# Gated attention, ELU layer and SwiGLU layer on one core: the first two chunks of layer one divided in halves, and the positive part of ELU made by ScalarE

## The chip, the cores and the metric

The kernel runs on one core of a Trainium2 chip, as one program launched once. The metric is device time in microseconds (us), the median over runs of the same program. The engines of the core are named as in the profile: PE (TensorE's matrix products), PEld (its weight loads), DVE (VectorE), ACT (ScalarE), POOL (GpSimd) and SP (SyncE, whose queue issues every DMA here).

## What is computed

Three stages follow one another, all in float32:

```
for t in range(S):                                   # attention, B=4, H=8, S=768, D=48
    state = alpha[t][:, None] * state + outer(k[t], v[t])
    y[t]  = q[t] @ state
x = y as 3072 tokens x 384
h = x @ w_in                                         # layer one, 384 -> 2048 -> 384
x = where(h > 0, h, exp(min(h, 0)) - 1) @ w_out
g = x @ w_gate                                       # layer two, 384 -> 1536 -> 384
out = (g * sigmoid(g) * (x @ w_val)) @ w_out2
```

## The kernel before

Tokens are worked on in six chunks of 512 (128 steps of the sequence for each of four batches). Attention is cut into 24 units, one for each chunk and batch, so four units make the input x of one chunk. The seven steps of a unit u stand in a list called `queue`, in the order A(u+1), E(u), N(u+1), Gs(u), M(u+1), Hy(u), Dk(u+1), and `pop(n)` emits the next n of them. The last one of a unit that writes x is Hy (lines 291 to 321; ACT lines 317 and 318 copy the high part, DVE lines 319 and 320 make the low part). After the fourth unit of a chunk, `gaps` moves rows of x with six small DMAs (x<-x, line 337), and only then is x complete. Unit u+3 is loaded when unit u is done, since there are three input buffers. After the first chunk, Dk, Gs and Hy of all units share one PSUM bank (`aps`).

Layer one of a chunk has 16 steps f, one for each 128 hidden features. `mm1(f)` multiplies x by a column block into a PSUM tile h (two buffers), in nine matmuls, since each float32 product is made of three passes over parts split in two. ELU then runs as a chain: ACT relu of -h (L361), ACT exp (L362), DVE minus one (L363), DVE max(h, 0) plus that (L364), ACT copy to the high part g (L366), DVE subtraction to the low part (L367). `mm2(f)` multiplies g into the three accumulators acc0 to acc2, again nine matmuls; it is emitted two steps late, through `pend`. After f=15 the accumulators are copied by ACT, DVE and ACT (L383, L381) into tiles o and stored to DRAM, from where layer two reads them.

Each of the 16 weight blocks of layer one arrives packed, is decoded by `value` (two ACT, two DVE operations, L91 to L98) and split by `split` (one ACT, one DVE, L105 and L106). `p1.step()` emits the split of one block and the decoding of the next; a raw block's load waits for the split that frees one of two buffers. `mm1(f)` and `mm2(f)` use blocks 2(f//2) and 2(f//2)+1. Before layer one starts, the four units of chunk 0 are emitted with three steps of `p1` among them; then one step follows each f of chunk 0:

```
for c in range(NCH):
    for f in range(NF1):
        mm1(f)
        pend.append((mm2, f))
        if c == 0:
            p1.step()
        ...
        pop(POPS[f])          # POPS = [3] * 9 + [1] + [0] * 6: 28 a chunk, the four units of chunk c+1
        if len(pend) > 2:
            m, ff = pend.pop(0)
            m(ff)
```

The program's order is not the engines' order: a planner places the instructions of all engines by their readiness in its own timing, the earlier emitted first among those that are ready, and the order on each engine is then fixed. Layer two's 18 weight blocks are prepared in the same way from the end of chunk 4 on, during chunk 5 and the first chunk of layer two.

Of the kernel before, what the change touches and what calls it, by code (L numbers as in the profile page):

```python
# [33 lines left out]
EARLY = 10  # L34
POPS = [3] * 9 + [1] + [0] * 6
PASSES = ((0, 0), (0, 1), (1, 0))
# [3 lines left out]
def kernel(  # L40
# [14 lines left out]
    def open_pools(es, weights):  # L55
        P.wp = es.enter_context(tc.tile_pool(name="wp", bufs=weights))
        P.xp = es.enter_context(tc.tile_pool(name="xp", bufs=2))
        P.ep = es.enter_context(tc.tile_pool(name="ep", bufs=2))
        P.gp = es.enter_context(tc.tile_pool(name="gp", bufs=3))
        P.rp = es.enter_context(tc.tile_pool(name="rp", bufs=AHEAD))  # L60
        P.op = es.enter_context(tc.tile_pool(name="op", bufs=2))

    dp = ctx.enter_context(tc.tile_pool(name="dp", bufs=1, space=bass.MemoryType.DRAM))
    x2d = [dp.tile([128, KD, TB], F32, name=f"x2d{c}") for c in range(NCH)]

# [57 lines left out]
    class Attention:  # L123
# [167 lines left out]
        def Hy(self, u):  # L291
# [11 lines left out]
            for p, cs in enumerate(cols):  # L303
# [6 lines left out]
                    start=not c and p == 0, stop=p == NP - 1,  # L310
                )
            x = xt[c]
            ts = slice(b * C, (b + 1) * C)
# [33 lines left out]

    def moe1(x, w1, pacc, ph, put):

# [3 lines left out]
        def mm1(f):  # L353
# [3 lines left out]
            for kk in range(KD):  # L357
                mm3(h, lambda a: w[:, a, kk, fs], lambda b: x[:, b, kk], kk == 0, kk == KD - 1)
            e = P.ep.tile([128, TB], F32, tag="e", name="e")
            g = P.gp.tile([128, 2, TB], F32R, tag="g", name="g")  # L360
            nc.scalar.activation(out=e, in_=h, func=AF.Relu, scale=-1.0)  # L361
            nc.scalar.activation(out=e, in_=e, func=AF.Exp, scale=-1.0)  # L362
            nc.vector.tensor_scalar(out=e, in0=e, scalar1=-1.0, scalar2=None, op0=ALU.add)  # L363
            nc.vector.scalar_tensor_tensor(  # L364
                out=e, in0=h, scalar=0.0, in1=e, op0=ALU.max, op1=ALU.add)
            nc.scalar.activation(out=g[:, 0], in_=e, func=AF.Copy)  # L366
# [4 lines left out]
        def mm2(f):  # L371
            w = as_rows(w1[f // G, 1])
            g = gh.pop(f)
            for m in range(KD):
                mm3(acc[m], lambda a: w[:, a, f % G, m * 128:(m + 1) * 128],
                    lambda b: g[:, b], f == 0, f == NF1 - 1)
            if f == NF1 - 1:
                for m in range(KD):
                    o = P.op.tile([128, TB], F32, tag="o", name="o")
                    if m == 1:  # L380
                        nc.vector.tensor_copy(o, acc[m])  # L381
                    else:
                        nc.scalar.activation(out=o, in_=acc[m], func=AF.Copy)  # L383
                    nc.sync.dma_start(out=put(m), in_=o)
# [99 lines left out]
    for u in range(NU):  # L484
# [3 lines left out]
        def finish(u=u):  # L488
            c, b = divmod(u, B)
            if b == B - 1:  # L490
                at.gaps(c, 0, B)
                if c + 1 < NCH:
                    new_x(c + 1)
            if u + 3 < NU:
# [24 lines left out]
    at.init()  # L519
    new_x(0)  # L520
    at.A(0)
# [3 lines left out]
    for i in range(B):  # L525
        pop(7)
        if i:
            p1.step()

    pend = []  # L530
    for c in range(NCH):
        mm1, mm2 = moe1(xt[c], w1, pacc, ph, lambda m, c=c: x2d[c][:, m])
        for f in range(NF1):
            mm1(f)
            pend.append((mm2, f))
            if c == 0:
                p1.step()
            if p2 and f * EARLY // NF1 < (f + 1) * EARLY // NF1:
                p2.step()
            pop(POPS[f])  # L540
            if len(pend) > 2:
                m, ff = pend.pop(0)
                m(ff)
            if c == NCH - 1 and f == 4:
                x_next = load_split(lambda m: x2d[0][:, m])
# [182 lines left out]
```

## Time and profile before

| | us |
|---|---|
| median of three runs | 1021.77 (1021.47 to 1023.0) |
| the profiled execution, device time | 1022.64 |
| its span, first to last instruction | 1020.9 |
| PE busy in the span | 980.6 |
| DVE busy | 573.5 |
| ACT busy | 462.7 |
| mean granted clock of PE, share of full speed | 0.974 |

The span and the device time differ by 1.7 us, and the profiled execution stands 0.87 us above the median. A busy PE is not a PE at its peak, since the ends of matmuls are modelled; the spacing of starts and the number of matmuls say more.

### The profile page before, as it was taken

How to read it: one execution, taken by the hardware profiler on the slowest of the kernel's cores; microseconds unless marked ns; L12 is line 12 of the kernel's file. 1: busy time of each engine (PE TensorE's matmuls, PEld its weight loads, DVE VectorE, ACT ScalarE, POOL GpSimd, SP SyncE). 2: the span in 40 equal slices, each digit the busy share in tenths (PEclk: the TensorE clock that was granted, in tenths of full speed). 3: DMA queues.
4: the chain of work that ended last, by engine and by line, in shares of the span. 5: the costliest groups of instructions: out<-in, count | busy, mean ns of one | idle time of the engine just before them, and what ended most of it. 6: DMA issues, size and time to landing. Idle time of an engine off the chain costs nothing.

```text
span 1020.9 us, 13174 instructions
## 1 busy us (share of the span) xinstructions
PE 980.6 (96%) x5248; PEld 813.9 (80%) x5248; DVE 573.5 (56%) x951; ACT 462.7 (45%) x806; POOL 86.2 (8%) x59
## 2 busy tenths in 40 slices
PE   7589999999999999999998999999999999999997
PEld 4467778877787878888776888888888888888886
DVE  6899996656665665647888433433433433433332
ACT  5678786455555455637877321211311222212121
POOL 4223111120211121100000000000000000000000
PEclk8589999999999999999999999999999999999998
DMA  5544432222112212203533100100200100100001
GB/s 227 206 160 165 165 120 74 83 57 73 43 55 75 83 42 58 73 16 125 186 124 125 62 1 1 62 1 1 62 1 1 62 1 1 62 1 22 10 0 35
DMA packets 18934, 69.36 MB, mean 68 GB/s; under 512 B 2480, under 2 KB 5552, under 8 KB 15920
## 3 DMA queue, kind: packets, MB, share of 16 engines
q1 hardware_dynamic: 18864, 68.43, 19.9%
q8 instruction: 43, 0.70, 0.3%
q14 instruction: 27, 0.22, 0.1%
HBM read 56.62 MB, written 9.44 MB: 65 GB/s over the span
## 4 chain that ended last, share of the span: by engine, by line
PE 79%; DVE 8%; DMA 7%; ACT 3%; issue 2%; SPq 0%; POOL 0%; DVEq 0%
PE gv L117 29%; PE q L117 15%; PE acc L117 14%; PE h L117 14%; DMA raw<-w 4%; DMA in<-qkva 2%; PE ape L254 2%; DVE wt L106 2%; PE aps L299 2%; PE aps L308 1%; DVE raw L98 1%; DVE raw L95 1%; DVE in L195 1%; ACT raw L93 1%; ACT raw L91 1%
## 5 line engine op out<-in xcount | busy, mean ns | idle before, releaser
L117 PE MATMUL gv<-x,wt 128*128 128x512 f32 x1296 | 310.1, 393 | 2.3 <-DVE e L364 2.3
L117 PEld LDWEIGHTS gv<-x,wt 128*128 128x128 f32 x1296 | 243.3, 189 | 51.0 <-issue 2.7
L117 PE MATMUL acc<-g,wt 128*128 128x512 f32 x864 | 224.6, 398 | 4.3 <-DVE g L367 2.4
L117 PE MATMUL h<-x,wt 128*128 128x512 f32 x864 | 220.3, 398 | 8.4 <-DVE e L364 4.2
L117 PEld LDWEIGHTS h<-x,wt 128*128 128x128 f32 x864 | 161.3, 190 | 45.5 <-DVE e L364 6.6
L117 PEld LDWEIGHTS acc<-g,wt 128*128 128x128 f32 x864 | 158.7, 188 | 44.0 <-DVE g L367 4.4
L117 PE MATMUL q<-wt,u 128*128 128x384 f32 x864 | 163.0, 337 | 0.0
L117 PEld LDWEIGHTS q<-wt,u 128*128 128x128 f32 x864 | 153.6, 188 | 5.5
L414 DVE TENSOR_TENSOR s<-gv,s 128x512 f32<-128x512 f32 x72 | 49.8, 692 | 180.9 <-ACT s L413 180.8
L413 ACT ACTIVATE s<-gv 128x512 f32<-128x512 f32 x72 | 43.1, 598 | 185.3 <-PE gv L117 185.2
L416 ACT ACTIVATE u<-s 128x512 fp32r<-128x512 f32 x72 | 45.4, 631 | 130.4 <-DVE s L415 130.4
L366 ACT ACTIVATE g<-e 128x512 fp32r<-128x512 f32 x96 | 60.2, 629 | 65.6 <-DVE e L364 64.1
L361 ACT ACTIVATE e<-h 128x512 f32<-128x512 f32 x96 | 56.7, 590 | 58.7 <-PE h L117 57.8
L367 DVE TENSOR_TENSOR g<-e,g 128x512 fp32r<-128x512 f32 x96 | 67.8, 708 | 16.5 <-ACT g L366 15.0
L363 DVE TENSOR_SCALAR e<-e 128x512 f32<-128x512 f32 x96 | 42.6, 446 | 61.2 <-ACT e L362 61.0
L417 DVE TENSOR_TENSOR u<-s,u 128x512 fp32r<-128x512 f32 x72 | 49.8, 692 | 44.0 <-ACT u L416 44.0
L415 DVE TENSOR_TENSOR s<-gv,s 128x512 f32<-128x512 f32 x72 | 49.8, 691 | 43.0 <-PE gv L117 43.0
L364 DVE SCALAR_TENSOR_TENSOR e<-h,e 128x512 f32<-128x512 f32 x96 | 65.9, 687 | 2.1
L224 POOL TENSOR_TENSOR in<-in 112x512 f32<-112x512 f32 x24 | 40.6, 1691 | 300.2 <-DVE in L195 266.5
L362 ACT ACTIVATE e<-e 128x512 f32<-128x512 f32 x96 | 59.9, 628 | 1.8
L195 DVE TENSOR_TENSOR_SCAN in<-in,zero 112x128 f32<-112x128 f32 x96 | 34.5, 415 | 26.8 <-DMA in<-qkva 26.8
L214 POOL TENSOR_TENSOR in<-in,R 112x512 f32<-112x512 f32 x24 | 43.6, 1818 | 35.7 <-ACT R L204 35.6
(88 smaller groups left out, 776.0 us busy)
## 6 DMA issues: line engine op xcount, KB each, us to landing
raw<-w SPq DMA_DIRECT2D x34, 768.0 KB, 4.3
in<-qkva SPq DMA_DIRECT2D x23, 1024.0 KB, 5.0
x2d<-o SPq DMA_DIRECT2D x18, 256.0 KB, 2.0
x2r<-x2d SPq DMA_DIRECT2D x18, 256.0 KB, 2.9
out<-y SPq DMA_DIRECT2D x24, 192.0 KB, 2.0
x<-x SPq DMA_DIRECT2D x36, 64.0 KB, 4.5
in<-qkva SPq DMA_DIRECT2D x1, 768.0 KB, 5.1
in<-qkva SPq DMA_DIRECT2D x1, 256.0 KB, 3.7
```

The lines of the kernel that those rows point to most:

```text
L117: nc.tensor.matmul(out=o, lhsT=lhs(a), rhs=rhs(b), start=first and i == 0, stop=last and i == 2,)
L195: nc.vector.tensor_tensor_scan(out=f, data0=f, data1=self.zero[0:PR].to_broadcast([PR, C]), initial=1.0, op0=ALU.mult, op1=ALU.add,)
L214: nc.gpsimd.tensor_tensor(out=k, in0=k, in1=d["R"], op=ALU.mult)
L361: nc.scalar.activation(out=e, in_=h, func=AF.Relu, scale=-1.0)
L362: nc.scalar.activation(out=e, in_=e, func=AF.Exp, scale=-1.0)
L364: nc.vector.scalar_tensor_tensor(out=e, in0=h, scalar=0.0, in1=e, op0=ALU.max, op1=ALU.add)
L366: nc.scalar.activation(out=g[:, 0], in_=e, func=AF.Copy)
L367: nc.vector.tensor_tensor(out=g[:, 1], in0=e, in1=f32(g[:, 0]), op=ALU.subtract)
L414: nc.vector.tensor_tensor(out=e, in0=ps[0], in1=e, op=ALU.mult)
L415: nc.vector.tensor_tensor(out=e, in0=ps[1], in1=e, op=ALU.mult)
L416: nc.scalar.activation(out=g[:, 0], in_=e, func=AF.Copy)
L417: nc.vector.tensor_tensor(out=g[:, 1], in0=e, in1=f32(g[:, 0]), op=ALU.subtract)
```

## The change

The work of layer one is cut into segments. Chunk 0's steps f=0 to 7 come first, then chunk 1's f=0 to 7, then chunk 0's f=8 to 15, then chunk 1's f=8 to 15, then chunks 2 to 5 whole. A segment that ends at f=7 stores its three accumulators to a DRAM tile `half`; the segment that ends at f=15 loads them into three o tiles when f=12 is reached, and DVE adds the accumulators to them before the store. The four units of chunk 1 are emitted in the first segment, four steps for each of seven f; the second and third segment have none; the units of chunk 2 come in the fourth. One step of `p1` follows each f of the first four segments, and two, not three, come before layer one. x of a chunk is allocated at its first Hy. In ELU, ACT makes relu(h) into a tile r (one buffer), the DVE operation L363 is gone, and L364 reads r and e in SBUF instead of h in PSUM. The o tiles get a third buffer.

```diff
-POPS = [3] * 9 + [1] + [0] * 6
+HALF = NF1 // 2
+FULL = [3] * 9 + [1] + [0] * 6
+SEGMENTS = [(0, 0, HALF, [4] * 7 + [0]), (1, 0, HALF, [0] * 8),
+            (0, HALF, NF1, [0] * 8), (1, HALF, NF1, [4] * 7 + [0])]
+SEGMENTS += [(c, 0, NF1, FULL) for c in range(2, 6)]
...
-        P.op = es.enter_context(tc.tile_pool(name="op", bufs=2))
+        P.op = es.enter_context(tc.tile_pool(name="op", bufs=3))
...
+    half = [dp.tile([128, KD, TB], F32, name=f"half{c}") for c in range(2)]
...
+            if b == 0:
+                new_x(c)
...
+            r = P.ep.tile([128, TB], F32, tag="r", name="r", bufs=1)
             nc.scalar.activation(out=e, in_=h, func=AF.Relu, scale=-1.0)
+            nc.scalar.activation(out=r, in_=h, func=AF.Relu)
             nc.scalar.activation(out=e, in_=e, func=AF.Exp, scale=-1.0)
-            nc.vector.tensor_scalar(out=e, in0=e, scalar1=-1.0, scalar2=None, op0=ALU.add)
             nc.vector.scalar_tensor_tensor(
-                out=e, in0=h, scalar=0.0, in1=e, op0=ALU.max, op1=ALU.add)
+                out=e, in0=e, scalar=-1.0, in1=r, op0=ALU.add, op1=ALU.add)
...
-                    lambda b: g[:, b], f == 0, f == NF1 - 1)
-            if f == NF1 - 1:
+                    lambda b: g[:, b], f == f0, f == f1 - 1)
+            if f == f1 - 1:
                 for m in range(KD):
-                    o = P.op.tile([128, TB], F32, tag="o", name="o")
-                    if m == 1:
+                    o = part[m] if part else P.op.tile([128, TB], F32, tag="o", name="o")
+                    if part:
+                        nc.vector.tensor_tensor(out=o, in0=acc[m], in1=o, op=ALU.add)
+                    elif m == 1:
...
-        if i:
+        if i > 1:
             p1.step()
...
-    for c in range(NCH):
-        mm1, mm2 = moe1(xt[c], w1, pacc, ph, lambda m, c=c: x2d[c][:, m])
-        for f in range(NF1):
+    for c, f0, f1, pops in SEGMENTS:
+        to = half[c] if f1 < NF1 else x2d[c]
+        part = []
+        mm1, mm2 = moe1(xt[c], w1, pacc, ph, lambda m, to=to: to[:, m], f0, f1, part)
+        for f in range(f0, f1):
...
-            if c == 0:
+            if c < 2:
                 p1.step()
...
-            pop(POPS[f])
+            pop(pops[f - f0])
...
+            if f0 and f == f0 + 4:
+                for m in range(KD):
+                    t = P.op.tile([128, TB], F32, tag="o", name="part")
+                    nc.sync.dma_start(out=t, in_=half[c][:, m])
+                    part.append(t)
```

## Rows read from the trace of the kernel before

**Rows 1.** The page's part 1: busy us of each engine over the span.

```profile
PE 980.6 (96%) x5248; PEld 813.9 (80%) x5248; DVE 573.5 (56%) x951; ACT 462.7 (45%) x806; POOL 86.2 (8%) x59
```

**Rows 2.** Windows: stretch, length; busy us (instructions) PE, PEld, DVE, ACT, POOL; clock, DMA.

```profile
56.00:156.00 100.00, 96.43 (x577) 75.81 (x578) 93.85 (x153) 79.07 (x137) 20.62 (x11) 0.96 0.45 154
242.00:328.00 86.00, 86.00 (x529) 68.54 (x529) 53.69 (x102) 46.66 (x91) 13.92 (x8) 1.00 0.20 63
470.00:570.00 100.00, 92.34 (x386) 72.21 (x385) 79.94 (x116) 77.29 (x116) 0.00 (x0) 0.98 0.37 129
```

**Rows 3.** Timeline of ACT, the chunks' first copy of acc0: start, duration, instruction.

```profile
156.00 0.60 ACT L383 ACTIVATE o<-acc 128x512 f32<-128x512 f32 x1
...
240.65 0.60 ACT L383 ACTIVATE o<-acc 128x512 f32<-128x512 f32 x1 [0.22 <-PE acc L117]
...
326.73 0.60 ACT L383 ACTIVATE o<-acc 128x512 f32<-128x512 f32 x1 [0.23 <-PE acc L117]
```

**Rows 4.** Timeline of PE: layer one's first matmuls, and four groups in chunk 1.

```profile
56.09 2.90 PE L117 MATMUL h<-x,wt 128*128 128x512 f32 x6 [3.93 <-DMA x<-x]
...
197.61 2.23 PE L117 MATMUL h<-x,wt 128*128 128x512 f32 x9
199.68 2.20 PE L117 MATMUL acc<-g,wt 128*128 128x512 f32 x9
201.72 2.20 PE L117 MATMUL h<-x,wt 128*128 128x512 f32 x9
203.76 0.39 PE L117 MATMUL acc<-g,wt 128*128 128x512 f32 x1
```

**Rows 5.** Windows of tile e alone: busy us of DVE, of ACT; clock, DMA.

```profile
56.00:156.00 100.00, 31.38 (x51) 31.22 (x52) 0.96 0.45 154
```

**Rows 6.** Windows of tile raw alone (weight blocks): busy us of DVE, of ACT.

```profile
56.00:156.00 100.00, 36.05 (x37) 30.76 (x35) 0.96 0.45 154
```

**Rows 7.** Windows of tile wt alone, before layer one: PE, PEld, DVE (x splits), ACT.

```profile
0.00:56.00 56.00, 0.00 (x0) 0.00 (x0) 4.70 (x5) 4.58 (x5) 0.67 0.55 201
```

**Rows 8.** Page, part 5: busy us, mean ns; then idle time before the group.

```profile
L361 ACT ACTIVATE e<-h 128x512 f32<-128x512 f32 x96 | 56.7, 590 | 58.7 <-PE h L117 57.8
...
L363 DVE TENSOR_SCALAR e<-e 128x512 f32<-128x512 f32 x96 | 42.6, 446 | 61.2 <-ACT e L362 61.0
...
L364 DVE SCALAR_TENSOR_TENSOR e<-h,e 128x512 f32<-128x512 f32 x96 | 65.9, 687 | 2.1
```

**Rows 9.** Timeline of DVE: the last operation of a unit, units 0, 3, 7, 8, 11.

```profile
20.77 0.54 DVE L320 TENSOR_TENSOR x<-aps,x 112x384 fp32r<-112x384 f32 x1
...
52.67 0.55 DVE L320 TENSOR_TENSOR x<-acc,x 112x384 fp32r<-112x384 f32 x1
...
135.78 0.55 DVE L320 TENSOR_TENSOR x<-aps,x 112x384 fp32r<-112x384 f32 x1
...
161.57 0.55 DVE L320 TENSOR_TENSOR x<-aps,x 112x384 fp32r<-112x384 f32 x1
...
218.67 0.55 DVE L320 TENSOR_TENSOR x<-aps,x 112x384 fp32r<-112x384 f32 x1
```

**Rows 10.** Waits of PE over the span: who for whom, us in total, times, longest.

```profile
PE h L117 <- DVE e L364: 4.2, 4, 1.6
...
PE acc L117 <- DVE g L367: 2.4, 4, 0.8
...
PE gv L117 <- DVE e L364: 2.3, 1, 2.3
PE acc L117 <- DVE o L381: 1.3, 1, 1.3
```

**Rows 11.** Waits of PE from 260 us on.

```profile
PE h L117 <- DVE e L364: 1.6, 2, 1.1
```

**Rows 12.** Timeline of SP: DMA issues, with the time that their waits took.

```profile
27.44 15.63 SPq L83 DMA_DIRECT2D raw<-w  x3
43.17 0.37 SPq L186 DMA_DIRECT2D in<-qkva  x1
```

More of the change, by code (lines that the diff above doesn't have):

```diff
@@ L345, in new_x, with moe1 @@
         xt[c] = P.xp.tile([128, 2, KD, TB], F32R, tag="x", name="x")
-    def moe1(x, w1, pacc, ph, put):
+    def moe1(x, w1, pacc, ph, put, f0=0, f1=NF1, part=()):
         acc = [pacc.tile([128, TB], F32, tag=f"acc{m}", name=f"acc{m}") for m in range(KD)]
@@ L491, in finish @@
                 at.gaps(c, 0, B)
-                if c + 1 < NCH:
-                    new_x(c + 1)
             if u + 3 < NU:
@@ L519 @@
     at.init()
-    new_x(0)
     at.A(0)
```

## The prediction

> **What bounds the kernel now.** I read the page's sums first, then windows of three kinds of stretch, then the chunks' ends, then the units of attention, then the waits. PE is busy 980.6 of 1020.9 us [rows 1], so nearly all time can only be won where PE has too little to do. Three stretches differ [rows 2]. In chunk 2 (242 to 328) PE is busy all 86.0 us, with DVE at 53.69 and ACT at 46.66: PE is the bound. In chunk 0 (56 to 156) DVE is busy 93.85 of 100 us, and in the preparation of layer two's weights (470 to 570) DVE and ACT are at 79.94 and 77.29, while PE falls to 96.43 and 92.34.
>
> How much PE loses in chunk 0 is not seen from its busy time, so I count. Three groups of nine matmuls start between 197.61 and 203.76, 2.05 us each [rows 4]. A whole chunk takes 326.73 - 240.65 = 86.1 us [rows 3]; its 32 groups are 65.6 us of that, so four units of attention cost PE 20.5 us. From the first matmul of layer one (56.09) [rows 4] to chunk 0's first copy of acc0 (156.00) [rows 3] lie 99.9 us. In them PE does 18 mm1 (two are of chunk 1), 15 1/3 mm2 and four units: 33.3 x 2.05 + 20.5 = 88.8. So **chunk 0 loses 11.1 us**, and with chunks 1 to 3 at PE's rate that is the largest sum within reach. DVE's 93.85 us there are 31.38 for e [rows 5], 36.05 for weight blocks [rows 6] and 26.4, the rest, for attention.
>
> **The first segment.** PE now has 16 groups and four units before it needs x of chunk 1: 32.8 + 20.5 = 53.3 us, from 56.1 to 109.4. x must come by then; before, it had the whole chunk.
>
> DVE's work until that x is done: ELU costs it 31.38 / 17 = 1.85 us a step now (51 instructions of e, three a step) [rows 5]; without L363's 0.446 [rows 8] it is 1.40, and eight steps are 11.2. The operation L364 stays at 0.687, the value I take though it now reads SBUF only. Attention is 26.4. A weight block takes three operations of 36.05 / 37 = 0.97, so 2.92 [rows 6]. The program has emitted ten steps by the end of the segment; five blocks are split before 56 us already, although only three steps are emitted by then [rows 7]. So five more are left: 14.6. The sum is 52.2 us, to 108.3. From a chunk's last DVE operation to PE's start on it passed 56.09 - 53.22 = 2.9 us [rows 4, 9]. By DVE's work x is ready at 111.2, and the loss is **1.8 us**. That is the lower bound.
>
> The upper one is from the spacing of units. Units 3 to 7 end 83.1 us apart, 20.8 each, while PE is filled with layer one; units 0 to 3 come 31.9 us apart, 10.6 each, while PE has nothing else [rows 9]. If the first two units keep the long spacing, and the last two the short one because PE has run out of matmuls, unit 7 ends at 52.7 + 41.6 + 21.2 = 115.5, x is ready at 118.9, and the loss is **9.5 us**. The traces are as near to one as to the other (DVE nearly full speaks for the first, two chunks' spacing for the second), so I take the middle, 5.6. **Gain in chunk 0: 11.1 - 5.6 = 5.5 us**, between 1.6 and 9.3.
>
> **The fourth segment.** Chunk 2's four units now have seven steps and no six empty ones behind them. From the copy of acc0 that ends the third segment, PE has 6 mm1, 8 2/3 mm2 and four units: 14.7 x 2.05 + 20.5 = 50.6 us. Unit 8 ended 5.6 us after such a copy, and units 8 to 11 come 57.1 us apart, 19.0 each [rows 3, 9]. At the spacing that DVE's sum gives above, (108.3 - 53.2) / 4 = 13.8, x of chunk 2 is there at 5.6 + 41.4 + 3.4 = 50.4: no loss. At 19.0, 19.0 and 10.6 it is there at 57.6: 7.0 lost. Queued behind that wait are all matmuls of chunk 2, since PE runs them in a fixed order; only the last two mm2 can be put ahead, and I have counted them. Middle: **3.5 us lost**.
>
> **Two more ends of segments.** Each adds three copies, three stores, later three loads and three DVE additions. The copies hide behind the mm1 that follows (2.05 us); of six ends now one shows a wait, 1.3 us [rows 10]. Two more cost 2 x 1.3 / 6 = **0.4 us**, at most 2.6. The stores pass through SP's queue, where raw loads now wait up to 15.63 us and the input of a unit waits behind them [rows 12]. After the first segment no unit's input is urgent, so I cost the DMAs at nothing; should a store hold up a raw load, the blocks concerned are not used until the third segment, a segment later.
>
> **ELU's engines.** ACT gains 96 x 0.590 = 56.6 us and DVE loses 96 x 0.446 = 42.8 [rows 8], neither on the path where PE is the bound. What can show is PE's waits. h is free after both relu now, not after relu, exp, L363 and L364: PE waited 4.2 us for that, 1.6 of it after chunk 0 [rows 10, 11], and 2.3 us where layer two's gv takes over the PSUM [rows 10]. At most 3.9 us come back. On the other side g comes later by 0.590 - 0.446 = 0.14 us and by ACT's queue; its waits are 2.4 us [rows 10], and I let them double as the other bound. r has one buffer, so ACT waits there for DVE's L364 of the step before, with exp and the weight blocks' copies behind it; a step lasts two groups, 4.1 us, which covers that unless DVE is full. Taken: **1.5 us gained**, from -2.4 to 3.9.
>
> **One step fewer ahead of layer one** is 2.92 us of DVE at most, but the planner splits five blocks there where three steps are emitted [rows 7], so it fills gaps in any case: nothing, up to 2.9. Allocating x at its first Hy moves no instruction.
>
> **Sum.** 5.5 - 3.5 - 0.4 + 1.5 = 3.1 us gained on an execution of 1022.64: 1019.5. That execution stood 0.87 above the median, so the median should be **1018.7**.
>
> **Rivals.**
>
> *The units of attention come too late.* One mechanism: x1 and x2 are chains of units, and more pops for each f don't shorten a chain that waits for itself. For it: the spacing is 20.8 us with DVE full and 19.0 with DVE at 62%, where the program's order, 2 1/3 steps a unit, would make it 2 1/3 x (4.1 + 20.5 x 3/28) = 14.7; it is longer at either load. Against it: 10.6 us with PE empty. With one spacing s in both segments the losses are 4s - 53.3 and 3s - 41.6, and with the other terms' 1.1 the gain is nil at s = 15.3; each microsecond more costs 7. At 16.5 the kernel is 8.4 us slower, **1030**. The forecast amounts to s = 14.7 in the first segment, not far off.
>
> *The gain is given back.* What chunk 0 loses is the latency of its first steps, not DVE's sum, and it stays; the weights now spread over a stage where PE was the bound anyway. Then 1.5 - 0.4 is left: **1021**. For it: the order on the engines is the planner's, and five splits against three steps show that moving a step in the program need not move it. Against it: DVE at 93.85 of 100 us.
>
> *ACT becomes the bound in the preparation of layer two's weights.* In 470 to 570 there are at most 92.34 / 4.10 = 22 steps; ACT goes from 77.29 to 90.3 us of 100, DVE from 79.94 to 70.1. It decides once ACT's queue, not DVE's, holds g. If PE's 2.4 us of waits for g tripled, the 1.5 us gained become 4.8 lost: **1025**. The Trainium skill says so as a rule (page "ScalarE: Activation LUTs", section "Rules for kernel authors": relu and max go to VectorE, not ScalarE); the trace agrees in that the operation added (590 ns) is longer than the one removed (446 ns) [rows 8].
>
> *All of it works*: the first bound in both segments, 9.3 - 0 - 0.4 + 1.5: 10.4 gained, **1011**.
>
> **Chances and range.** Forecast 0.43 (its own range 1014 to 1022), late units 0.28, given back 0.17, ACT 0.05, all of it 0.07. About 0.2%, or 2 us, is what a measurement of this kernel can tell from no change: faster is below 1019.7, slower above 1023.8. Faster: 0.36 + 0.07 + 0.03 = 0.46. Same: 0.06 of the forecast, 0.13 of the second rival, 0.05 of the others = 0.24. Slower: 0.30, nearly all late units. The range 1010 to 1030 leaves out the later half of the late units and a little of the best case, 0.16.
>
> **What the profile after would show.** Right: the first matmul of chunk 1 between 111 and 119 us with a wait for x<-x below some 6 us, unit 7's L320 near 112, DVE above 90% only until then; no PE wait for L364; at chunk 2's start a wait for x<-x of a few us. Wrong: units still 17 us or more apart in the first or fourth segment, with PE idle and its clock down ahead of chunk 1 or 2; PE waits for g in 470 to 570 above 5 us; or the wait at L364 replaced by one of equal length for r.

## The result, and the profile after

The changed kernel takes 1035.53 us (median, 1034.06 to 1036.17), the kernel before 1022.38 beside it: a ratio of 1.0125, with a 95% interval of 1.0107 to 1.0143. It is slower by 13 us, where 3 us of gain were predicted. The profiled execution has a span of 1034.4 us, 13.5 more than before.

PE's sums on the page hardly differ from [rows 1]; DVE has 25.6 us less and ACT 39.0 us more to do, the way that the change says, though less than the 42.8 and 56.6 us that the prediction took. On ACT consecutive operations overlap in the trace: three of one chain start at 224.82, 225.31 and 225.79 and take 0.6 us each, so one more adds less than its 0.59 us:

```profile
PE 982.6 (95%) x5248; PEld 820.0 (79%) x5248; DVE 547.9 (53%) x861; ACT 501.7 (49%) x902; POOL 87.8 (8%) x59
```

The waits of PE (who for whom, us in total, times, longest) answer to [rows 10, 11]. The wait of h for DVE's L364 is gone, but PE now waits for x three times (once before, ahead of chunk 0), and for two operations of attention ahead of chunks 1 and 2:

```profile
PE h L122 <- DMA x<-x: 8.4, 3, 3.8
...
PE aps L240 <- DVE x L327: 5.2, 1, 5.2
PE acc L122 <- ACT g L375: 4.0, 4, 2.5
PE aps L304 <- DVE T L292: 3.5, 2, 3.0
```

Where these waits lie, the timeline of PE shows (start, duration, instruction, idle time before it and its releaser). The three h are the first matmuls of chunks 0, 1 and 2, and answer to the first of [rows 4]:

```profile
56.86 2.90 PE L122 MATMUL h<-x,wt 128*128 128x512 f32 x6 [3.76 <-DMA x<-x]
...
126.54 0.98 PE L240 MATMUL aps<-ident,in 112*128 112x112 f32 x4 [5.22 <-DVE x L327]
...
129.36 2.90 PE L122 MATMUL h<-x,wt 128*128 128x512 f32 x6 [1.84 <-DMA x<-x]
...
253.80 1.63 PE L304 MATMUL aps<-in,sbd 112*112 112x128 f32 x8 [3.04 <-DVE T L292]
...
264.96 4.38 PE L122 MATMUL h<-x,wt 128*128 128x512 f32 x12 [2.79 <-DMA x<-x]
```

With the prediction's rate the losses can be counted. PE had 53.3 us of work for the first segment and took 129.36 - 56.86 = 72.5: **19.2 us lost** ahead of chunk 1. From there to chunk 2 it had 48 groups of 2.05 us and four units, 118.9 us, and took 264.96 - 129.36 = 135.6: **16.7 us lost**. Before, chunk 0 lost 11.1. The difference, 24.8 us, is what the changed kernel loses there against the one before; some 12 us come back elsewhere. Of the 19.2 us the profile names 5.2 and 1.8 us for attention and x, as shown, and 5.4 us for ELU's g (3.6 for ACT's, 1.8 for DVE's).

The windows (stretch, length; busy us and instructions of PE, PEld, DVE, ACT, POOL; clock, DMA share, GB/s) show both gaps and PE's clock in and behind them:

```profile
56.00:126.00 70.00, 58.46 (x384) 45.21 (x384) 63.26 (x98) 55.68 (x102) 17.65 (x9) 0.89 0.53 186
116.00:126.00 10.00, 4.86 (x46) 3.63 (x44) 7.40 (x12) 7.09 (x14) 2.54 (x2) 0.84 0.63 221
126.00:136.00 10.00, 7.62 (x35) 5.59 (x36) 8.61 (x14) 6.92 (x12) 3.37 (x2) 0.50 0.69 196
246.00:256.00 10.00, 6.96 (x53) 5.57 (x55) 5.88 (x10) 4.27 (x9) 2.98 (x2) 0.91 0.21 79
256.00:266.00 10.00, 5.15 (x53) 4.12 (x50) 4.10 (x11) 1.70 (x5) 0.62 (x1) 0.67 0.54 144
480.00:580.00 100.00, 99.62 (x439) 81.36 (x438) 64.36 (x87) 81.68 (x135) 0.00 (x0) 1.00 0.34 114
```

After PE had been busy for 4.86 of 10 us, the granted clock was 0.50 of full speed, the lower level of 1.2 GHz, all through 126 to 136: six matmuls of h took 2.90 us there, nine take 2.2 at full speed [rows 4]. So part of the 16.7 us is the clock: 129.36 to 136 at half speed is, by estimate, 3.3 us. Part of the 19.2 us is the clock too: it was 0.50 from 112 to 116, behind a wait of 2.48 us for g that ended at 111.15. The last window answers to the third of [rows 2]: in the stretch where layer two's weights are prepared PE is now busy 99.62 of 100 us.

The units are why x is late. The timeline of DVE gives the last operation of a unit, as [rows 9] did; here units 3 to 11, and between units 8 and 9 (at 208.78) the addition of acc0 that ends the third segment:

```profile
53.43 0.55 DVE L327 TENSOR_TENSOR x<-acc,x 112x384 fp32r<-112x384 f32 x1
75.30 0.54 DVE L327 TENSOR_TENSOR x<-aps,x 112x384 fp32r<-112x384 f32 x1
93.99 0.54 DVE L327 TENSOR_TENSOR x<-aps,x 112x384 fp32r<-112x384 f32 x1
110.12 0.55 DVE L327 TENSOR_TENSOR x<-aps,x 112x384 fp32r<-112x384 f32 x1
125.85 0.54 DVE L327 TENSOR_TENSOR x<-aps,x 112x384 fp32r<-112x384 f32 x1
201.23 0.55 DVE L327 TENSOR_TENSOR x<-aps,x 112x384 fp32r<-112x384 f32 x1
...
208.78 1.38 DVE L390 TENSOR_TENSOR part<-acc,part 128x512 f32<-128x512 f32 x2 [1.46 <-PE acc L122]
...
222.93 0.55 DVE L327 TENSOR_TENSOR x<-aps,x 112x384 fp32r<-112x384 f32 x1
241.07 0.55 DVE L327 TENSOR_TENSOR x<-aps,x 112x384 fp32r<-112x384 f32 x1
258.77 0.55 DVE L327 TENSOR_TENSOR x<-aps,x 112x384 fp32r<-112x384 f32 x1
```

Units 3 to 7 end (125.85 - 53.43) / 4 = 18.1 us apart, units 8 to 11 (258.77 - 201.23) / 3 = 19.2. The prediction's first rival gives with these spacings 4 x 18.1 - 53.3 = 19.1 and 3 x 19.2 - 41.6 = 16.0 us of loss; 19.2 and 16.7 were counted. The first agreement is the mechanism: x was there 3.0 us after unit 7, as the formula has it. The second is partly luck. The formula lets unit 8 end 5.6 us after the end of the third segment, and it ended 7.6 us ahead of it (201.23 against 208.78). From 208.78 to chunk 2 it took 56.2 us, for which the prediction counted 50.6 of work; unit 8's quarter of the attention work (5.1 us) was done by then, so some 10.7 of the 16.7 us were lost behind that point. The other 6.0 fall ahead of it, the 3.3 of the clock among them. And x of chunk 2 was there 5.6 us after unit 11, not 2.9.

Unit 7 shows how DVE's load gets into the spacing. ACT had made its high part by 123.51, but DVE's fixed order put an operation of a weight block (L103, at 123.29 for 1.84 us) and one of a later unit (L217, 0.68 us) ahead of the low part, which started at 125.65: 2.1 us.

In the fourth segment DVE is far from full, and a unit's time can be followed on the one PSUM bank aps, first on PE, then on DVE (with ACT's copy of KT at 230.90 between Dk and Gs):

```profile
222.56 2.22 PE L122 MATMUL h<-x,wt 128*128 128x512 f32 x9
224.62 2.20 PE L122 MATMUL acc<-g,wt 128*128 128x512 f32 x9
226.66 1.52 PE L122 MATMUL h<-x,wt 128*128 128x512 f32 x6
228.02 0.55 PE L240 MATMUL aps<-ident,in 112*128 112x112 f32 x4
...
231.48 0.26 PE L279 MATMUL aps<-in,KT 128*64 128x48 f32 x1 [0.22 <-ACT KT L243]
...
236.97 1.04 PE L304 MATMUL aps<-in,sbd 112*112 112x128 f32 x8
```

```profile
235.26 0.35 DVE L292 TENSOR_TENSOR T<-aps,sc 112x192 f32<-112x192 f32 x1
241.07 0.55 DVE L327 TENSOR_TENSOR x<-aps,x 112x384 fp32r<-112x384 f32 x1
```

One unit leaves the bank at 222.93 + 0.55; the next one's Dk (L240), KT, Gs (L279), T (L292), Hy (L304) and x follow in turn, to 241.07. The operations of these that write or read the bank add up to about 6 us of the 18. Between them stands other work in PE's fixed order: Dk, for one, had the bank free from 223.5 on and came behind the 24 matmuls of layer one above. Its input was not what it waited for: the operation that completes a unit's k (L227) had run for all units up to 11 by 158.6.

Against this, ELU gave time back. The chunks' first copy of acc0, on ACT's timeline, continues [rows 3] for chunks 2 to 5. First the kernel before, then the one after:

```profile
326.73 0.60 ACT L383 ACTIVATE o<-acc 128x512 f32<-128x512 f32 x1 [0.23 <-PE acc L117]
...
413.30 0.60 ACT L383 ACTIVATE o<-acc 128x512 f32<-128x512 f32 x1
...
497.06 0.59 ACT L383 ACTIVATE o<-acc 128x512 f32<-128x512 f32 x1
...
569.43 0.60 ACT L383 ACTIVATE o<-acc 128x512 f32<-128x512 f32 x1 [0.68 <-PE acc L117]
```

```profile
352.14 0.60 ACT L394 ACTIVATE o<-acc 128x512 f32<-128x512 f32 x1
...
437.90 0.58 ACT L394 ACTIVATE o<-acc 128x512 f32<-128x512 f32 x1
...
517.49 0.61 ACT L394 ACTIVATE o<-acc 128x512 f32<-128x512 f32 x1
...
584.46 0.58 ACT L394 ACTIVATE o<-acc 128x512 f32<-128x512 f32 x1
```

Chunk 2 ends 25.4 us later than before, and from there to the end of the span the changed kernel is 11.9 us faster (682.3 against 694.2 us): chunks 4 and 5 take 79.6 and 67.0 us instead of 83.8 and 72.4.

### The profile page after: what moved, and what is told of

It reads as the page before. It is cut to its first block, busy times and chain, and to the rows that moved or that the text cites. A ratio compares the mean times of both kernels' runs of the same rounds, so it can differ in the third digit from the quotient of the medians.

```text
span 1034.4 us, 13191 instructions
## 1 busy us (share of the span) xinstructions
PE 982.6 (95%) x5248; PEld 820.0 (79%) x5248; DVE 547.9 (53%) x861; ACT 501.7 (49%) x902; POOL 87.8 (8%) x59
## 4 chain that ended last, share of the span: by engine, by line
PE 81%; DVE 7%; DMA 6%; ACT 3%; issue 1%; POOL 0%; SPq 0%; DVEq 0%; POOLq 0%; ACTq 0%
PE gv L122 27%; PE h L122 16%; PE acc L122 16%; PE q L122 14%; DMA in<-qkva 3%; DMA raw<-w 2%; PE ape L259 2%; PE aps L304 2%; PE aps L313 1%; DVE in L200 1%; DVE raw L103 1%; DVE raw L100 1%; DVE wt L111 1%; DMA x<-x 1%; DVE A L266 1%
## 5 line engine op out<-in xcount | busy, mean ns | idle before, releaser
L122 PE MATMUL h<-x,wt 128*128 128x512 f32 x864 | 223.8, 401 | 8.4 <-DMA x<-x 8.4
L122 PEld LDWEIGHTS h<-x,wt 128*128 128x128 f32 x864 | 164.6, 193 | 45.0 <-ACT R L208 4.0
L373 DVE SCALAR_TENSOR_TENSOR e<-e,r 128x512 f32<-128x512 f32 x96 | 68.1, 709 | 76.7 <-ACT e L372 76.5
L370 ACT ACTIVATE e<-h 128x512 f32<-128x512 f32 x96 | 56.9, 592 | 66.9 <-PE h L122 65.5
L229 POOL TENSOR_TENSOR in<-in 112x512 f32<-112x512 f32 x24 | 43.7, 1821 | 316.2 <-DVE in L200 305.3
L371 ACT ACTIVATE r<-h 128x512 f32<-128x512 f32 x96 | 56.6, 590 | 0.0
L100 DVE SCALAR_TENSOR_TENSOR raw<-raw 128x768 int32<-128x768 int32 x34 | 33.9, 996 | 25.6 <-ACT raw L98 25.5
```

The source lines that it names most:

```text
L122: nc.tensor.matmul(out=o, lhsT=lhs(a), rhs=rhs(b), start=first and i == 0, stop=last and i == 2,)
L371: nc.scalar.activation(out=r, in_=h, func=AF.Relu)
L373: nc.vector.scalar_tensor_tensor(out=e, in0=e, scalar=-1.0, in1=r, op0=ALU.add, op1=ALU.add)
```

## The experiments

Two theories were set against each other for the loss, and three for ELU. **A**: the units come 18 to 19 us apart whatever the program's order asks, so x can't be ready in half a pass. **B**: the first segment is overfull with weight work on DVE and ACT, or the division itself (ends, stores, loads, additions, x allocated late) costs. For ELU: h is released earlier, or the chain to g is shorter, or the new order that the planner makes from any edit is lucky. Kernels under one heading ran on one chip, beside the same runs of the kernel before; a ratio is always to those.

### The two parts apart, and two ways to ease ELU or the units

**elu_only**: the kernel before with the new activation alone.

```diff
+            r = P.ep.tile([128, TB], F32, tag="r", name="r", bufs=1)
             nc.scalar.activation(out=e, in_=h, func=AF.Relu, scale=-1.0)
+            nc.scalar.activation(out=r, in_=h, func=AF.Relu)
...
-            nc.vector.tensor_scalar(out=e, in0=e, scalar1=-1.0, scalar2=None, op0=ALU.add)
             nc.vector.scalar_tensor_tensor(
-                out=e, in0=h, scalar=0.0, in1=e, op0=ALU.max, op1=ALU.add)
+                out=e, in0=e, scalar=-1.0, in1=r, op0=ALU.add, op1=ALU.add)
```

> The kernel before with the ELU part of the change alone (relu(h) by ACT into r, L363 gone), segments and pops as before. Theory 1 (the segments cost some 25 us because the units of attention stay 18 to 19 us apart, and the ELU part gives back some 11 us where DVE and ACT prepare layer two's weights): about 1011 us, chunk 5 near 67 us instead of 72.4, hardly any PE wait for h after chunk 0. Theory 2 (ScalarE's extra operation is what made the changed kernel slow): 1025 us or more.

Measured: 1005.94 us, ratio 0.9825 (0.9773 to 0.9877), 5 us better than the first theory said. Chunk 5 took 66.8 us.

**segments_only**: the changed kernel with these lines taken back.

> The changed kernel with the ELU chain of before (L363 kept, max by DVE), all the segments kept. Theory 1: about 1046 us, units of chunk 1 and 2 some 18 to 20 us apart, PE waiting for x of chunk 1 and of chunk 2. Theory 2 (the ELU part is what cost the time, the segments gain): 1020 us or less.

Measured: 1054.18 us, ratio 1.0285 (1.0239 to 1.033), 8 us above the 1046 expected. So the segments cost 29.6 us with the new activation (1035.53 - 1005.94) and 31.8 without, and the activation is worth 16.4 us by itself and 18.7 beside the segments. The units came 19.5 us apart in the first segment.

**fold_only**: the kernel before with its minus one folded into the copy and the subtraction that follow: one DVE operation fewer, none more on ACT, and h still released by DVE.

```diff
-            nc.vector.tensor_scalar(out=e, in0=e, scalar1=-1.0, scalar2=None, op0=ALU.add)
...
-            nc.scalar.activation(out=g[:, 0], in_=e, func=AF.Copy)
-            nc.vector.tensor_tensor(
-                out=g[:, 1], in0=e, in1=f32(g[:, 0]), op=ALU.subtract)
+            nc.scalar.activation(out=g[:, 0], in_=e, func=AF.Copy, bias=-1.0)
+            nc.vector.scalar_tensor_tensor(
+                out=g[:, 1], in0=e, scalar=-1.0, in1=f32(g[:, 0]), op0=ALU.add, op1=ALU.subtract)
```

> The kernel before, with one DVE operation fewer in ELU and none more on ACT: the minus one goes into ACT's copy to g (bias -1) and into DVE's subtraction, so h is still freed by DVE, after exp. If the gain of the ELU part comes from DVE's lighter load: about 1011 us, as with r. If it comes from ACT freeing h earlier: above 1017 us, with the PE waits for h at the max operation still there.

Measured: 1011.63 us, ratio 0.9879 (0.9834 to 0.9924): 10.7 us gained, with 3.4 us of waits of h for DVE left (4.2 before). The edit lightens DVE, shortens the way to g and frees h one operation sooner; which of the three counts it does not separate.

**fast_pops**: the kernel before with the steps of the units taken four to an f.

```diff
-POPS = [3] * 9 + [1] + [0] * 6
+POPS = [4] * 7 + [0] * 9
```

> The kernel before with pops of 4 in each of seven steps, then none, in all chunks; nothing else. Theory 1 (a unit waits for its own chain, not for the program's pops): the last DVE operations of the units of chunk 2 still come 18 to 20 us apart, and the time stays within 0.3% of before. Rival (the pops set the pace): they come some 14 us apart.

Measured: 1018.40 us, ratio 0.9951 (0.9929 to 0.9973). Units 8 to 11 came 19.4 us apart (19.0 before) and units 12 to 15 18.2 (19.1 before), where the program's order asks for units a quarter fewer groups apart. The rate written in the program does not set the spacing. The time is 4.0 us (0.5%) lower all the same, more than the 0.3% allowed for; why was not followed.

### The units' bank, the weight blocks, and the early release of h

**after_gs_ape**: the changed kernel with Gs of units 4 and later in the PSUM pair of E, out of the bank that Dk and Hy use.

```diff
-            o = self.bank(u)
+            o = self.bank(u) if u < B else self.pair(1)[0]
```

> The changed kernel with one edit: Gs of a unit after the first chunk writes into the first bank of the ape tile (that of E) instead of the aps bank, which Dk and Hy then share alone. Theory A (units are spaced by the chain of Dk, Gs and Hy through one PSUM bank, with the queues of PE, ACT and DVE between): the spacing falls from 18 to 19 us to 13 or 14 in the first and the fourth segment, PE's wait ahead of chunk 1 and chunk 2 nearly goes, time 1010 to 1020 us. Theory B (DVE's sum of work spaces them in the first segment): the spacing there stays near 18 us and at best the fourth segment gains, time 1028 or more.

Measured: 1032.28 us, ratio 1.0092 (1.0072 to 1.0112). The units came 16.1 us apart in both segments. Both of A's numbers, 13 or 14 us and 1010 to 1020, were missed, and B's spacing near 18 too. Chunk 2 began at 252.75, 12.2 us earlier, but chunk 1 at 128.25, only 1.1 earlier, though unit 7 was done 8.0 us earlier. Unit 7's end on DVE, and chunk 1's first matmul on PE:

```profile
117.90 0.55 DVE L327 TENSOR_TENSOR x<-aps,x 112x384 fp32r<-112x384 f32 x1
```

```profile
128.25 6.71 PE L122 MATMUL h<-x,wt 128*128 128x512 f32 x27 [1.31 <-DMA x<-x]
```

Between them lie 9.8 us, against 3.0 in the changed kernel. The six small DMAs that complete x, issued from 118.24 on, landed 7.4 to 9.5 us after their issue; in the changed kernel it was 2.4 to 3.1. Two raw blocks of 768 KB and an input of 1 MB had been issued between 115.4 and 118.2, and the DMA engines were busy 0.99 of the time from 118 to 124 (0.67 in the changed kernel from 126 to 132). PE filled that time with unit 8's Dk, Gs, Hy and E, which stood ahead of chunk 1 in its order (to 126.9, 2.4 us of it a wait for KT), and then waited 1.31 us for x. So here chunk 1 no longer started by unit 7, but by those DMAs and by what PE's order had put ahead. Part of what was won by chunk 2's start was lost again in the pass of chunk 2, which ended 5.7 us earlier.

**after_gate**: the changed kernel with the loads of the raw blocks 10 to 15 held until chunk 1's last unit, by a POOL copy of one element of its x into the raw tile.

```diff
+            if gate is not None:
+                nc.gpsimd.tensor_copy(self.raw[0:1, 0:1, 0].bitcast(F32), gate)
...
+            gate = f32(xt[1][0:1, 1, 2, TB - 1:TB]) if i >= 10 and P.gated else None
```

> The changed kernel in which the loads of weight blocks 10 to 15 wait for the last unit of chunk 1 (a one-element copy by POOL from that unit's x into the raw tile ahead of each load), so that these blocks can't be decoded in the first segment, where nine were split against the five that it needs. Theory B (DVE's sum): four blocks of 2.92 us less before x of chunk 1, so it comes some 12 us earlier, time near 1025 us. Theory A (chain through one bank): x comes at most 4 us earlier, time 1031 to 1036 us, unless the late blocks then delay the third segment.

Measured: 1032.27 us, ratio 1.0092 (1.0072 to 1.0112). The windows of this run, and of its tile raw alone (DVE, ACT, POOL), over the same 70 us as above:

```profile
56.00:126.00 70.00, 58.15 (x406) 45.48 (x407) 55.61 (x93) 49.00 (x93) 19.27 (x12) 0.91 0.43 143
```

```profile
56.00:126.00 70.00, 14.43 (x15) 11.38 (x13) 0.29 (x2) 0.91 0.43 143
```

DVE fell from 63.26 to 55.61 us, and chunk 1 began at 125.32, 4.0 us earlier. Unit 7's last operation came at 120.54, 5.3 us earlier, and the units 16.8 us apart. So B is a part, some 3 us of the time: an eighth less on DVE brought the units 7% closer. DVE being full is not all that spaces them.

**keep_only**: the kernel before with relu(h) by ACT, and DVE still with its two operations (minus one, and e plus r): h is released early, DVE saves nothing.

```diff
+            nc.scalar.activation(out=r, in_=h, func=AF.Relu)
...
-            nc.vector.scalar_tensor_tensor(
-                out=e, in0=h, scalar=0.0, in1=e, op0=ALU.max, op1=ALU.add)
+            nc.vector.tensor_tensor(out=e, in0=e, in1=r, op=ALU.add)
```

> The kernel before with relu(h) made by ACT into r, as in the change, but with the minus-one operation on DVE kept (DVE then adds e and r in SBUF): h is freed early by ACT, DVE has as many operations as before, ACT one more. If the earlier release of h is worth the difference between the ELU part alone (1005.9) and the variant with one DVE operation fewer but h freed by DVE (1011.6): 1014 to 1018 us. If only DVE's lighter load counts: 1022 us or more.

Measured: 1015.17 us, ratio 0.9918 (0.9901 to 0.9935). The early release alone is worth 8.3 us, the operation fewer, with what else fold_only's edit does, 10.7, and the new activation with both 16.4: both count.

**elu_gs_ape**: the kernel before with the new activation and Gs in the pair of E, as the base for after_gs_ape.

> The kernel before with the ELU part of the change and Gs in the bank of ape; no segments. Theory A: units of a chunk 13 to 14 us apart, but x is not waited for in whole chunks, so the time is within 0.4% of the ELU part alone, 1002 to 1010 us.

Measured: 1020.37 us (1013.88 to 1023.66), ratio 0.9969 (0.9952 to 0.9987), a miss of the 1002 to 1010 expected: beside the new activation the move of Gs costs 14 us by itself, and its executions spread widely. Beside it the segments cost 11.9 us by the medians and 18.1 by the profiled spans (1030.2 against 1012.1), not 29.6. So with units 16.1 us apart the segments' cost falls by 11 to 18 us. A's formula gives 17 (2.0 and 3.1 us of spacing less make 4 x 2.0 + 3 x 3.1), but the starts do not bear it out place by place: it asks for chunk 1 to start 8 us earlier and chunk 2 17, and they started 1.1 and 12.2 earlier.

### The interleave undone

**half_in_order**: the changed kernel with all of its divisions, but with the halves in order, and the units at their old rate over a whole pass.

```diff
-SEGMENTS = [(0, 0, HALF, [4] * 7 + [0]), (1, 0, HALF, [0] * 8),
-            (0, HALF, NF1, [0] * 8), (1, HALF, NF1, [4] * 7 + [0])]
+SEGMENTS = [(0, 0, HALF, FULL[:8]), (0, HALF, NF1, FULL[8:]),
+            (1, 0, HALF, FULL[:8]), (1, HALF, NF1, FULL[8:])]
...
-        if i > 1:
+        if i:
             p1.step()
```

> The changed kernel with the four half passes put back in order: chunk 0's first half, chunk 0's second half, then chunk 1's two halves, with the units of attention at 3 per group over 9 groups as before the change. So the division, the two more chunk ends, the trip of the partial sums through DRAM and the new activation all stay; only the interleave is undone. Theory A (the loss is that units 18 to 20 us apart can't be finished inside a half pass of some 50 to 70 us): a chunk's eight units have a whole pass again, so PE waits for no x between chunks, and the kernel falls to that with the new activation alone and the price of two more ends, 1006 to 1011 us. Rival (the division itself costs: ends, stores, loads and additions): it stays above 1020 us.

Measured: 1009.68 us, ratio 0.9885 (0.985 to 0.9921), 25.9 us less than the changed kernel. A chunk has four units, not the eight of the expectation. PE waits 1.95 us for x ahead of chunk 1, at 148.03, and not at all ahead of chunk 2. Chunk 2's end, on ACT's timeline:

```profile
324.13 0.60 ACT L394 ACTIVATE o<-acc 128x512 f32<-128x512 f32 x1
```

In the changed kernel it was at 352.14, 28.0 us later; the rest of the two spans is the same, 682.3 us (1006.4 - 324.13 and 1034.4 - 352.14). So what the interleave costs lies ahead of that point, and it is the whole of the loss: with the halves in order this kernel is faster than the one before by 1.15%. The rate of the units and the one early step of `p1` are undone along with it; by themselves they cost no time (fast_pops, before_late_step).

**elu_fast_pops**: elu_only with the POPS of fast_pops.

> The kernel before with the new activation and with the steps of attention taken four to a group over 7 groups, not three over 9. The rate written in the code gained 4 us on the kernel before. If the two gains have different causes (PE waiting for the activation in every group; the last units of a chunk ending close to the chunk's end) they add: 1002 us. If both came from the same wait ahead of a chunk's first group, which the new activation no longer shows, 1006 us, as without it.

Measured: 1005.35 us, ratio 0.984 (0.9814 to 0.9865): the same as elu_only. The 4 us of fast_pops are not added to the activation's gain. This is the fastest kernel of the study, with elu_only, and its range is the narrower one.

**elu_o3**: elu_only with the third o buffer (`bufs=3` of the pool op).

> The kernel before with the new activation and the third buffer for o, which the change also brought. The wait of the copies for an o buffer was 1.3 us in all in the trace of before, so both theories expect nothing: 1004 to 1007 us. A gain of 3 us or more would say that the buffer is a part of the change's own that the other runs left out.

Measured: 1011.36 us, ratio 0.9893 (0.9862 to 0.9923): no gain, and 5 us above elu_only by the medians and above the 1007 expected, while the two intervals share 0.9862 to 0.9877. What these 5 us are, if they are, stayed open. half_in_order, which has the buffer too and ran beside it, is 3.7 us above elu_only, so the division with the buffer costs no more than the buffer alone.

**after_gs_gate**: after_gs_ape and after_gate together.

> The changed kernel with both aids together: the Gs products of the later units in the other PSUM pair (spacing 16.1 us by itself, 3 us gained) and the raw loads of blocks 10 to 15 held back until chunk 1's last unit (3 us gained). Theory A (spacing of the units sets the loss, 7 us for one us of spacing over both late places): the spacing in the first segment falls below 16 us, and the time to 1022 to 1028 us. Theory B (the two gain the same thing, room on DVE and ACT in the first segment): 1031 us, no better than either alone.

Measured: 1029.26 us, ratio 1.0065 (1.0042 to 1.0089). The units came 15.2 and 16.0 us apart, chunk 1 began at 116.39 and chunk 2 at 247.26, 13.0 and 17.7 us earlier than in the changed kernel. Neither theory's time came true. By the medians the two aids add up (3.3 us each, 6.3 together), though the interval overlaps those of the single ones; by chunk 1's start (1.1, 4.0 and 13.0 us earlier) they do not gain the same thing. With the raw loads held back the six small DMAs landed 2.3 to 2.5 us after their issue. The first segment now loses 116.39 - 55.73 - 53.3 = 7.4 us, less than chunk 0 did before (11.1). Of the 17.7 us the median keeps 6.3; chunk 2's pass alone gave back 6.1 (it ended 11.6 us earlier).

### What a new order is worth by itself

Each edit makes the planner write another order for PE, so elu_only holds that effect too. Three more kernels without the new activation were run to size it.

**before_o3**: the kernel before with the third o buffer.

> The kernel before with a third buffer for o, and nothing else. The planner writes another order of PE's matmuls for any edit, so the gain of the new activation holds the effect of a new order too. If an order by itself is worth little, this kernel stays at 1022 us within 3, and the 16 us belong to the activation. If the third buffer or a new order costs some 5 us, as beside the new activation, 1027 us.

Measured: 1021.79 us, ratio 0.9991 (0.9967 to 1.0015).

**before_late_step**: the kernel before with two, not three, steps of `p1` ahead of layer one (`if i > 1:`).

> The kernel before with two, not three, steps of the weight preparation ahead of layer one: another small part of the change by itself, and a second sample of a new order. The prediction put it at nothing, up to 2.9 us gained: 1019 to 1022 us. An order worth more than that by itself would show as a difference of 5 us or more to either side.

Measured: 1022.56 us, ratio 0.9993 (0.9974 to 1.0013).

**half_old_elu**: half_in_order with the old activation.

> The half passes in order, with the old activation: division, DRAM trip and third o buffer alone. With the interleave as the cause of the loss, 1022 to 1027 us, and the new activation is worth 13 to 17 us here too, as it was beside both other orders. If the activation's 16 us were luck of an order, the difference to the 1009.7 us with the new one would be under 8 us.

Measured: 1022.94 us, ratio 1.001 (0.9989 to 1.0031). Three other orders, one of them quite different, and the time stays within 0.1%. Beside the old activation the division with its ends, its trip through DRAM and its additions costs nothing that can be measured, and the activation is worth 13.3 us here too (1022.94 against 1009.68). A fourth order, fast_pops, did move the time, by 4.0 us.

## Why the prediction was wrong, step by step

The step that failed is "the traces are as near to one as to the other ..., so I take the middle" for the spacing of units, in both late segments: the units stayed 18.1 and 19.2 us apart, and PE lost 24.8 us more ahead of chunks 1 and 2 where 2.0 of gain were forecast. The second is the term for ELU's engines, whose direction was right and whose size was a tenth.

| term | predicted, us | measured, us | shown by |
|---|---|---|---|
| loss ahead of chunk 1 (chunk 0's before: 11.1) | 5.6 | 19.2 | timeline of PE |
| loss ahead of chunk 2 | 3.5 | 16.7 | timeline of PE |
| the two together, against before | 2.0 gained | 24.8 lost; 28.0 against the same halves in order | half_in_order |
| two more ends of segments | 0.4 lost | nothing beside the old activation; with the third o buffer 3.7 beside the new one, intervals overlapping | half_old_elu, half_in_order |
| ELU | 1.5 gained | 13 to 19 gained | elu_only, segments_only, half_old_elu |
| one step fewer ahead of layer one | nothing | nothing | before_late_step |

**The first segment.** Both of its bounds were wrong. The lower one, DVE's sum, counted five blocks (ten steps hold ten decodings but nine splits, so by its own rule 13 operations or 12.7 us were left, not 14.6); the windows of tile raw over 56 to 126 show 26 operations of it on DVE, about nine blocks:

```profile
56.00:126.00 70.00, 26.03 (x26) 21.59 (x26) 0.89 0.53 186
```

The kernel before has 27 of them (26.27 us) in the same 70 us. So emitting the steps later in the program did not move them on DVE; that is what the prediction's second rival had warned of. The sum of the other terms held: 11.2 + 26.4 + 26.0 = 63.6 us, and DVE was busy 63.26, though ELU took 12.64 of it and the rest 24.6. With that count and this order x would have come no earlier than 56.9 + 63.6 + 2.9 = 123.4, and the lower bound of the loss had been 13, not 1.8. The upper bound let the last two units take the short spacing of an empty PE; they took 16.1 and 15.7 us. And the middle between them had no ground: a spacing of 20.8 with DVE full and of 19.0 with DVE at 62% [rows 2, 9] is a spacing that DVE's load does not set by itself, which the text noted under the rival and did not use in the sum. after_gate bears that out: an eighth off DVE's load moved unit 7 by 5 us out of 72. So DVE's load is a part of the spacing, and the bank another (Gs moved out of it, 16.1 us), and with both eased it was still 15.2.

**The fourth segment.** Here DVE's sum was no bound at all (5.88 of 10 us in 246 to 256), and the other end of the range, 7.0, let the last unit come 10.6 us after the one before it; it came 17.7. With the spacing of the kernel before, 19.0, for all three, the loss is 3 x 19.0 - 41.6 = 15.4. What I called a rival was what the rows said, though its sum for this place came near in part by luck: unit 8 was 13 us earlier than it assumed, and it left out the 6.0 us lost ahead of the third segment's end and 2.7 more in the trip of x's rows. At 19.0 us in both places its formula loses 22.7 + 15.4 us, which makes 1048, not 1030; with the 15 us that ELU gives beyond the 1.5 taken that is 1033, close to what came, and with the luck just named.

**Chunk 0's loss** was to be won by spreading the weights. They were not spread: up to 126 DVE did as much weight work as before, and PE came to wait for x. In elu_only chunk 0 takes 156.81 - 55.90 = 100.9 us, about as before (99.9). Some of it was there to be won: in after_gs_gate, with the raw loads held back and the units closer, the first segment lost 7.4 us, not 11.1, but 12.0 were lost from there to chunk 2.

**ELU.** The term was made from the waits that the profile names for PE, 3.9 us at most. The same count by rate that chunk 0 got would have shown more: chunk 5 has no units, so its 32 groups are 65.6 us of work, and it took 569.43 - 497.06 = 72.4: 6.8 us lost. Of them 5.2 us are named waits, 4.4 of these between 519 and 562; the last four, on PE's timeline of the kernel before:

```profile
536.72 0.97 PE L117 MATMUL acc<-g,wt 128*128 128x512 f32 x3 [0.50 <-ACT g L366]
538.47 1.64 PE L117 MATMUL acc<-g,wt 128*128 128x512 f32 x6 [0.79 <-DVE g L367]
...
555.44 3.69 PE L117 MATMUL acc<-g,wt 128*128 128x512 f32 x15 [0.30 <-DVE g L367]
561.42 6.62 PE L117 MATMUL gv<-x,wt 128*128 128x512 f32 x21 [2.28 <-DVE e L364]
```

In elu_only layer two's first matmuls start at 546.47, 15 us earlier, and one short wait is left there:

```profile
545.66 0.96 PE L117 MATMUL acc<-g,wt 128*128 128x512 f32 x3 [0.18 <-ACT g L367]
546.47 4.71 PE L117 MATMUL gv<-x,wt 128*128 128x512 f32 x20
```

Its chunks end at 156.81, 239.39, 323.64, 409.41, 489.13 and 555.96: against before, chunks 0 to 5 give -0.8, 2.1, 1.8, 0.8, 4.0 and 5.5 us, and what follows 2.2, together the 15.7 us between the spans. The last 2.2 are mostly where the mark falls: layer two's first matmul starts 8.0 us ahead of it before, 9.5 in elu_only. The rest of chunk 5's 6.8 us is the clock behind the wait of 2.28 us: it was 0.50 from 562 to 565, which by estimate costs 1.5 us. The windows of before and then of elu_only show it (0.96 and 1.00):

```profile
556.00:600.00 44.00, 41.72 (x190) 35.70 (x189) 21.14 (x32) 15.98 (x25) 0.00 (x0) 0.96 0.11 37
```

```profile
556.00:600.00 44.00, 44.00 (x214) 38.75 (x213) 30.28 (x41) 22.49 (x35) 0.00 (x0) 1.00 0.33 108
```

The causes are both parts of the edit: h released by ACT (keep_only) and one DVE operation fewer (fold_only). The planner's new order is part of each of these runs. Three other orders without the activation moved the time by 1 us at most and a fourth, fast_pops, by 4.0; beside it the third o buffer went with 5. So an order is unlikely to carry a gain of 13 to 19 us, but it can't be taken apart from it, and its size is known to some 5 us only.

**The rivals.** Late units came true, at more than its price. Of "given back" the time did not come true, but its mechanism did in part: the weight work stayed where it was. "All of it works" did not occur. ACT as the bound in the preparation of layer two's weights was wrong: in that stretch, 480 to 580 now, PE rose to 99.62 of 100 us with ACT at 81.68, not 90.3. The waits for ACT's g are 4.0 us over the span, 3.6 of them in the first segment. The rule that the prediction weighed with it (the Trainium skill, page "ScalarE: Activation LUTs", section "Rules for kernel authors": relu and max on VectorE) is right here on the operation, 590 ns on ACT for 446 saved on DVE, and wrong on the kernel: keep_only, which moves the positive part to ACT and saves DVE no operation, became 0.8% faster, and elu_only 1.75%. The measurement decides.

**What stays open.** That the interleave costs the time is shown, and that chunk 1 of the changed kernel started when unit 7's x had landed. Why the planner's order keeps some 18 us between units was followed in one unit, not tried: no run held PE's order fixed. What the move of Gs costs elsewhere (14 us by the medians), what the third o buffer does beside the new activation, and why fast_pops gained 4 us were not followed.

## What to carry to other kernels

Before a consumer's time is halved, read how far apart its producer's pieces come in the trace, at two loads of the engine that you suspect: a spacing that hardly moves (20.8 and 19.0 us here, at 94% and 62%) is not that engine's alone, and it goes into the sum as it stands, not as the middle to a bound that it never met. When pieces then come sooner, look at the DMAs that carry them: here 8.0 us won on the units became 1.1 at the consumer, since the rows of x shared the DMA engines with weight loads and a later unit's work stood ahead in PE's order. Count what PE loses in every stretch as its time less its work at full rate, the stretches that look full too; the named waits held 5.2 of 6.8 us in chunk 5, the clock behind them the rest, and the 3.9 us that the prediction drew from them were a quarter of what ELU was worth. When a change has two parts, price the small one with the same care: here it was worth 16 us alone, with the layer's order left as it was.

## What the runs showed of the hardware

Behind 10 us with PE busy for 4.86 the next 10 us, with PE busy for 7.62, ran at a granted clock of 0.50 (1.2 GHz), so the waits of 5.2 and 1.8 us ahead of chunk 1 cost, by estimate, about 3 more behind them. Six DMAs of 64 KB landed 2.4 to 3.1 us after their issue with the DMA engines 0.67 busy (126 to 132, the changed kernel), and 7.4 to 9.5 us with them 0.99 busy, behind three loads of 768 KB to 1 MB (118 to 124, after_gs_ape). An operation that is 144 ns longer on ACT than the one it replaces on DVE was no loss with ACT busy 81.68 of 100 us.
